# Moving GpSimd's k and q scalings, the FFN's weight sums and two k scalings in a fused attention and FFN kernel

## The chip, the cores and the metric

The kernel runs on one core of a Trainium2 chip. A core has a matrix engine (TensorE, PE in the profile, with its weight loads as PEld), a vector engine (VectorE, DVE), a scalar engine (ScalarE, ACT), a general engine (GpSimd, POOL) and a queue engine (SyncE, SP), each with an instruction stream of its own; they wait for one another through semaphores. The metric is the time of one execution on the device in microseconds (us).

## The reference

Inputs are q, k and v of 4 batches, 8 heads, 768 positions and 64 columns, a decay `lam` for each head, and three weight matrices. First comes an attention without softmax, whose weights decay with distance and whose state is carried from block to block:

```
for b in range(nb):                      # blocks of positions
    intra = (qb @ kb.T * Dmask) @ vb     # Dmask[i, j] = lam ** (i - j) for i >= j, else 0
    inter = (qb * lam_pow) @ kv_state
    out[block] = intra + inter
    kv_state = lam_block * kv_state + (kb * rev_pow).T @ vb
```

Its output, as x of 3072 tokens by 512 columns, goes through a bilinear feed-forward layer (FFN): `a = x @ w_a`, `b = x @ w_b` (512 by 1536 each), and the result is `(a * b) @ w_out` (1536 by 512).

## The kernel before

**Units and groups.** The work is cut into 24 units of 128 positions (4 batches, 6 blocks each). `GROUPS = (4, 2, 4, 4, 4, 4, 2)` says how many units make up one group; the FFN runs group by group. While the FFN of one group runs, the attention pieces of the next units are put between its matmuls.

**Attention of a unit.** Loads of q and k as float32 (`load_x`, line 143), of v as bfloat16 (`make_vb`, line 282, on GpSimd's queue). k and q are multiplied by powers of the decay (`make_ks`, `make_qs`, `scale`, line 266), which takes the place of the decay mask; for units 4 to 7 VectorE scales k, for later units GpSimd does, and q is always GpSimd's. `prep_k` (a step "P") does both scalings; from unit 10 on it also issues a transposing DMA on SP (line 291), calls `pump`, and the step issues the load of v. `pump` issues on SP the loads of q and k for units 10 and up, three units ahead, and first of all, once, waits on SP for v of unit 9 with a tiny copy (line 188). Units 4 to 9 are transposed by TensorE instead (`piece_T`, a step "T", line 302: eight transposes, q's four first, then k's four; ScalarE copies the result, line 304). `piece_S` ("S") computes scores (line 316) and multiplies them by a triangular mask on VectorE (line 333). `piece_V` ("V") and `kv_beside` add to the state (line 380, 402), and VectorE copies it (line 413). `pieces_O` ("O2", "Q") computes the output of two units (line 350), ScalarE writes it as x transposed (line 373), and for the last unit of a group `sums` follows.

**The FFN.** Group 0 uses `ffn`: for each of 12 blocks of 128 features, four matmuls for a, four for b, and a product a·b on VectorE (line 483); then the output matmuls (line 634) into four accumulators. The a blocks of features 8 to 11 are all computed before the first of their b blocks. Groups 1 to 6 use `ffn_seven`: a and b for two halves of the tokens are computed with seven products of half-size matrices instead of eight (line 524). That takes four sums of the weights for each of six column blocks (`w_sums`, a step "TW", lines 489 to 492, VectorE, both inputs in SBUF) and four sums of x for each group (`sums`, lines 502 to 505, VectorE, both inputs in SBUF). Snapshots of the accumulators go through ScalarE (line 539), sums over them through VectorE (558, 569, 575) and for some steps GpSimd (561), and the product a·b of one half of the tokens is GpSimd's (571), of the other VectorE's (578).

**The order.** The schedule is written by hand: the order of the calls is the order of each engine's instructions. `hook(slot)` is called at numbered places of each group's FFN and carries out the steps that `PLAN[group]` lists for that slot. In group 0, slots 0 to 11 come after each feature block's product, slots 12 to 35 after each pair of output matmuls. In the later groups, slots 0 to 11 lie between the seven-product steps, and slots from 12 on between the output matmuls. Slot 6 of group 1 comes after the group's third product of line 571; slot 1 of group 2 before the group's first product of line 571, slot 3 after it, slots 4 and 5 both between its second and third. A step "L" issues loads on GpSimd's queue. The outputs of groups 0 and 1 (units 0 to 5) are kept in SBUF (`o_kept`) and stored in group 2.

**Loads.** GpSimd issues first the weights in the order of `W_ORDER`, mixed with q, k and v of units 4 and 5, and later those of units 6 to 9 in steps "L". Each of its DMA issues keeps GpSimd for 0.7 to 0.9 us.

Of the kernel before, what the change touches and what calls it, by code (L numbers as in the profile page):

```python
# [17 lines left out]
BF16 = mybir.dt.bfloat16  # L18
# [4 lines left out]
def _bc(ap, dims):  # L23
# [19 lines left out]
W_ORDER = ("a0", "a1", "b0", "b1", "a2", "b2", "a3", "b3", "a4", "a5", "b4", "b5", "o0", "q4", "k4", "o1", "v4",  # L43
           "q5", "k5", "o2", "v5", "o3")
PLAN = {
    0: [(0, "V", 3), (1, "TW", 0), (3, "TW", 1), (5, "TW", 2), (7, "TW", 3),
        (9, "P", 4), (9, "L", ("q6", "k6", "o4")), (11, "P", 5), (11, "L", ("o5", "v6", "q7")),
        (12, "L", ("k7", "v7")), (13, "TW", 4), (14, "T", 4), (17, "S", 4), (17, "P", 6), (18, "T", 5),
        (18, "L", ("q8", "k8", "v8")), (21, "V", 4), (22, "S", 5), (23, "TW", 5), (24, "T", 6),
        (24, "L", ("q9", "k9")), (25, "P", 7), (25, "L", ("v9",)), (26, "O2", (4, 5)), (28, "S", 6), (31, "T", 7),  # L50
        (33, "P", 8)],
    1: [(0, "V", 6), (1, "S", 7), (2, "T", 8), (2, "P", 9), (4, "O2", (6, 7)),
        (5, "S", 8), (5, "T", 9), (7, "S", 9), (11, "V", 8), (12, "O2", (8, 9)), (14, "P", 10), (15, "P", 11)],
    2: [(1, "P", 12), (4, "P", 13), (7, "P", 14), (11, "S", 10), (11, "S", 11), (12, "P", 15),
        (14, "P", 16), (17, "P", 17)],
    3: [(4, "P", 18), (7, "P", 19), (13, "P", 20), (16, "P", 21)],
    4: [(4, "P", 22), (7, "P", 23)],
# [9 lines left out]
def kernel(  # L67
# [11 lines left out]
    nc = tc.nc  # L79
    B, H, S, D = q.shape  # L80
    BLK = 128
    NB = S // BLK
# [5 lines left out]
    KS = d_model // 128  # L88
# [3 lines left out]
    singles = ctx.enter_context(tc.tile_pool(name="singles", bufs=1))  # L92
    wst_pool = ctx.enter_context(tc.tile_pool(name="wst", bufs=13))
    ld_pool = ctx.enter_context(tc.tile_pool(name="ld", bufs=4))
    prep_pool = ctx.enter_context(tc.tile_pool(name="prep", bufs=6))
# [37 lines left out]
    raw = {}  # L133

    def load_x(w, u, queue):
        b, nb = divmod(u, NB)
        if u in (n0 + 4, n0 + 5):
            if (u, "kq") not in raw:
                raw[u, "kq"] = wst_pool.tile([128, 2, H, D], F32, name="qkf", tag="wst")
            t = raw[u, "kq"][:, "qk".index(w)]  # L140
        else:
            t = ld_pool.tile([128, H, D], F32, name=w + "f", tag=w + "f", bufs=4)
        queue.dma_start(out=t, in_={"q": qr, "k": kr}[w][b, nb])
        raw[u, w] = t
# [23 lines left out]
    n0 = GROUPS[0]  # L168
# [4 lines left out]
    def load_all(parts):  # L173
        for kind, c in parts:
            if kind in "abo":
                load_w(kind, int(c))
            elif kind == "v":
                make_vb(int(c))
            else:
                load_x(kind, int(c), nc.gpsimd)  # L180

    landed = singles.tile([1, 1], BF16, name="landed")

    def pump():
        if used["u"] < n0 + 6:
            return
        if used["u"] == n0 + 6:
            nc.sync.dma_start(out=landed, in_=U[n0 + 5]["vb"][0:1, 0, 0:1])
        while pending:
            w, u = pending[0]  # L190
            if u >= used["u"] + 3:
                return
            load_x(w, u, nc.sync)
            pending.pop(0)
# [15 lines left out]
    for w, src in (("q", q), ("k", k)):  # L210
# [3 lines left out]
        for c in range(0, HP, n_c):  # L214
            t = wst_pool.tile([128, 1024], F32, name=w + "4", tag="wst")[:, :n_c * 512]
            t = t.rearrange("p (c b x) -> p c b x", c=n_c, b=2)
# [28 lines left out]
    lp_q = singles.tile([128, NT, H, 1], F32, name="lp_q")  # L245
    lp_k = singles.tile([128, NT, H, 1], F32, name="lp_k")
# [12 lines left out]
    U = {}  # L259
    kv = {}  # L260

    def eng_of(name):
        return nc.gpsimd if name == "pool" else nc.vector

    def scale(eng, dst, x, lp):
        eng_of(eng).tensor_mul(dst.rearrange("p (c b) d -> p b c d", b=2),  # L266
                               x[:].rearrange("p (b c) d -> p b c d", b=2),
                               lp.rearrange("p (b c) o -> p b c o", b=2)
                               .to_broadcast([128, 2, HP, D]))

    def make_ks(u, eng):
        qk = prep_pool.tile([128, 2, H, D], BF16, name="qk", tag="qk")
        scale(eng, qk[:, 1], raw.pop((u, "k")), lp_k[:, u % NB])
        U.setdefault(u, {}).update(qk=qk, kn=qk[:, 1])

    def make_qs(u, eng):
        scale(eng, U[u]["qk"][:, 0], raw.pop((u, "q")), lp_q[:, u % NB])

    def make_vb(u):
        b, nb = divmod(u, NB)  # L280
        vb = prep_pool.tile([128, H, D], BF16, name="vb", tag="vb", bufs=8)
        nc.gpsimd.dma_start(out=vb, in_=vr[b, nb])  # L282
        U.setdefault(u, {})["vb"] = vb

    def prep_k(u):
        make_ks(u, "dve" if u < n0 + 4 else "pool")
        make_qs(u, "pool")
        used["u"] = u + 1
        if u in DMA_T:
            qkT = qkT_pool.tile([128, 2, HP, 128], BF16, name="qkT", tag="qkT")  # L290
            nc.sync.dma_start_transpose(
                out=qkT[:].rearrange("p j hp i -> p (j hp) i"),
                in_=U[u]["qk"][:].rearrange("p j h d -> p (j h d)"))
            U[u]["qT"], U[u]["kT"] = qkT[:, 0], qkT[:, 1]
        pump()
# [50 lines left out]
    def o_mm(u, b, c, **ops):  # L346
        h = 4 * b + c
        p = slice(64 * (h % 2), 64 * (h % 2) + 64)
        new = U[u]["flags"]
        nc.tensor.matmul(U[u]["o"][b][p, c // 2, :], start=new[b, h % 2], stop=True,  # L350
                         skip_group_check=True, **ops)
        new[b, h % 2] = False
# [8 lines left out]

    def intra(u, b):
        for c in range(HP):
            o_mm(u, b, c, lhsT=U[u]["vb"][:, 4 * b + c, :], rhs=U[u]["m"](b, c))

    def evac_o(us, b, eng="act"):
        xT, col = xTs[us[0]]
# [9 lines left out]
    def kv_mms(ps, w, cs, first):  # L377
        d = U[w]
        for c in cs:
            nc.tensor.matmul(ps[:, c, :, :], lhsT=d["kn"][:, 2 * c:2 * c + 2, :],  # L380
                             rhs=d["vb"][:].rearrange("p (b c) d -> p c b d", b=2)[:, c],
                             start=(first and c == 0), stop=True, skip_group_check=True)

    def kv_bank():
# [3 lines left out]
    def kv_update(u):  # L388
        if u % NB == NB - 1:
            return  # L390
        if u % NB == 0:
            kv_bank()
        kv_mms(kv["ps"], u, range(HP), u % NB == 0)

    def kv_beside(u):
        if u % NB == 0 or u % NB == NB - 1:
            kv_update(u)
            return
        for c in range(HP):
            for b in range(2):  # L400
                p = slice(64 * b, 64 * b + 64)
                nc.tensor.matmul(kv["ps"][p, c, b, :], lhsT=U[u]["kn"][:, 2 * c + b, :],
                                 rhs=U[u]["vb"][:, 4 * b + c, :],
                                 start=False, stop=True, skip_group_check=True)

    def kv_copy(u, ps, eng="dve"):
# [9 lines left out]
    def piece_S(u):  # L416
        masks(u, scores(u))
# [198 lines left out]
    def store_kept():  # L616
        row, o_sb = kept.pop(0)
        nc.sync.dma_start(out=out_r[row], in_=o_sb)
# [61 lines left out]
    def new_xT(g):  # L680
        gx[g] = xT_pool.tile([128, KS, 512], BF16, name="xT", tag="xT")
        for i in range(GROUPS[g]):
            xTs[g_u0[g] + i] = (gx[g], i * BLK)
# [62 lines left out]
    for u in range(n0):  # L746
        U[u] = dict(kn=kn4[:, u], qT=xT4["q"][:, :, u * BLK:(u + 1) * BLK],
                    m=lambda i, hp, u=u: ms4[hp // 2, u // 2][i][:, 2 * (u % 2) + hp % 2, :])
# [57 lines left out]
    bank["held"].clear()  # L806
    used["u"] = n0
    pump()

    for g, n in enumerate(GROUPS):  # L810
        if g + 1 < len(GROUPS):
            new_xT(g + 1)
        plan = {}
        for slot, name, us in PLAN.get(g, ()):
            plan.setdefault(slot, []).append((name, us))

        def hook(slot, plan=plan):
            for name, us in plan.get(slot, ()):
                if name == "P":
                    prep_k(us)  # L820
                    if us in DMA_T:
                        make_vb(us)
                elif name == "L":
                    load_all(us)
                elif name == "TW":
                    w_sums(us)
                elif name == "W":
                    store_kept()
                elif name == "T":
                    piece_T(us)  # L830
                elif name == "S":
                    piece_S(us)
                elif name == "V":
                    piece_V(us)
                elif name == "O":
                    pieces_O((us,))
                elif name == "O2":
                    pieces_O(us)
                else:
                    pieces_O(us[:2], us[2:])  # L840

        if g in S_GROUPS:
            ffn_seven(g, g_u0[g], n, gx.pop(g), hook, g + 1 == len(GROUPS))
        else:
            ffn(g_u0[g], n, gx.pop(g), hook, g == 0)
# [29 lines left out]
```

## Time and profile before

| What | Value |
|---|---|
| Median of 5 runs | 223.96 us (223.80 to 224.42) |
| Profiled execution, its time | 224.41 us |
| Profiled execution, its span | 222.4 us |
| TensorE busy | 216.0 us (97%) |
| VectorE busy | 154.5 us (69%) |
| GpSimd busy | 136.1 us (61%) |
| ScalarE busy | 104.8 us (47%) |

The profile is of one execution, and its times count from the start of the span. A line of a timeline gives the start, the duration, the engine, the line of the kernel, the operation, output and inputs by the program's names with their shapes, the number of instructions merged into the line, and in brackets how long the engine had been idle and what ended that. A line of waits gives who waited for whom: the sum in us, the number of times, the longest. Group 0's FFN runs from about 17.9 to 53.4 us, group 1's from there to 73.4, group 2's begins at 73.41.

### The profile page before, as it was taken

Reading aid. Unit: us, or ns where it says so; the run is one execution under the profiler, and the core shown is the slowest. Engines: PE = TensorE matmul, PEld = TensorE weight load, DVE = VectorE, ACT = ScalarE, POOL = GpSimd, SP = SyncE. Lnnn points to the kernel's source line nnn. Section 1 sums busy time; section 2 is a strip of 40 time slices with the busy share of each in tenths; the row PEclk is TensorE's granted clock in tenths of the full one; section 3 lists DMA queues with packets and bytes.
Section 4 is the critical chain, followed back from the end, with each engine's and each line's share of the span. In section 5 each row is a group of like instructions: output and inputs, shape, how many; then the busy total and the mean of one; then the engine's idle time right before and its main releaser. Section 6 shows DMA issues by size and latency. Waiting matters only on the chain.

```text
span 222.4 us, 5431 instructions
## 1 busy us (share of the span) xinstructions
PE 216.0 (97%) x2203; PEld 149.5 (67%) x2203; DVE 154.5 (69%) x250; ACT 104.8 (47%) x185; POOL 136.1 (61%) x150
## 2 busy tenths in 40 slices
PE   7899999999999899999999999999999999999994
PEld 2476444556985588754688754688754788745974
DVE  0992997899687987993677873577973687830760
ACT  2686233336862456324466424566324557342622
POOL 6879659996759869995169992169910246400230
PEclk9999999999999999999999999999999999999999
DMA  3999999996753999999977959506611200012102
GB/s 106 312 164 193 202 245 236 227 242 112 177 113 26 173 228 193 201 343 187 277 179 110 174 132 229 115 1 74 71 48 49 97 1 0 3 47 97 47 3 94
DMA packets 82858, 30.76 MB, mean 138 GB/s; under 512 B 70034, under 2 KB 79122, under 8 KB 82834
## 3 DMA queue, kind: packets, MB, share of 16 engines
q0 software_dynamic: 32864, 11.01, 44.2%
q1 hardware_dynamic: 49682, 19.34, 35.6%
q8 instruction: 17, 0.28, 0.5%
q10 hardware_dynamic: 288, 0.07, 0.1%
q14 instruction: 7, 0.06, 0.1%
HBM read 28.32 MB, written 6.29 MB: 156 GB/s over the span
## 4 chain that ended last, share of the span: by engine, by line
PE 88%; DMA 4%; DVE 2%; ACT 2%; SPq 1%; issue 1%; ACTq 0%
PE op L634 25%; PE m_q L524 23%; PE m_r L524 12%; PE m_p L524 6%; PE o_ps L350 5%; PE a_ps L456 5%; PE b_ps L456 5%; PE kq L316 3%; DMA k<-in_k_dram 3%; PE kvd L380 1%; PE tps L302 1%; SPq L218 1%; DVE xs L502 1%; DMA out_dram<-o_sb 1%; ACT o_kept L625 1%
## 5 line engine op out<-in xcount | busy, mean ns | idle before, releaser
L634 PE MATMUL op<-wo_sb,ab 128*128 128x512 bf16 (+2 forms) x312 | 68.1, 363 | 0.0
L571 POOL TENSOR_TENSOR ab<-c,c 128x512 bf16<-128x512 bf16 x30 | 34.8, 1164 | 36.4 <-DVE c L569 35.6
L524 PEld LDWEIGHTS <-tw 128*128 128x128 bf16 x576 | 49.1, 98 | 6.9 <-DVE xs L503 0.4
L634 PEld LDWEIGHTS <-ab 128*128 128x128 bf16 x312 | 27.6, 98 | 26.3 <-POOL ab L571 0.6
L524 PE MATMUL m_q<-xs,tw 128*128 128x256 bf16 (+1 forms) x288 | 36.1, 255 | 0.4 <-ACT s L539 0.2
L561 POOL TENSOR_TENSOR c<-s 128x512 bf16<-128x512 f32 x11 | 14.0, 1272 | 33.9 <-ACT s L539 33.9
L333 DVE TENSOR_TENSOR m<-kq,lotri 128x512 bf16<-128x512 f32 x47 | 29.8, 683 | 5.5 <-PE kq L316 4.9
L629 ACT COPY o_sb<-op 128x512 f32<-128x512 f32 (+2 forms) x20 | 10.9, 543 | 43.5 <-PE op L634 43.0
L578 DVE TENSOR_TENSOR ab<-c,m_q 128x512 bf16<-128x512 f32 x30 | 20.6, 686 | 11.7 <-PE m_q L524 9.8
L524 PEld LDWEIGHTS <-wa_sb 128*128 128x128 bf16 x288 | 24.5, 98 | 3.1
L539 ACT COPY s<-m_q 128x512 f32<-128x512 f32 x30 | 17.6, 588 | 15.7 <-PE m_q L524 14.6
L569 DVE TENSOR_TENSOR c<-u,m_r 128x512 f32<-128x512 f32 x30 | 20.4, 681 | 4.7 <-ACT u L539 4.6
L282 POOL DMA_DIRECT2D vb<-in_v_dram x24 | 22.3, 931 | 1.7 <-DMA wo_sb<-in_moe_w_out_dram 1.1
L558 DVE TENSOR_TENSOR c<-s,m_p 128x512 bf16<-128x512 f32 x19 | 13.0, 686 | 11.8 <-PE m_p L524 11.6
L575 DVE TENSOR_TENSOR c<-s,m_q 128x512 f32<-128x512 f32 x30 | 20.5, 685 | 0.5
L539 ACT COPY s<-m_r 128x512 f32<-128x512 f32 x30 | 17.7, 590 | 6.4 <-PE m_r L524 6.4
L539 ACT COPY u<-m_q 128x512 f32<-128x512 f32 x30 | 17.9, 597 | 5.6 <-PE m_q L524 5.6
L266 POOL TENSOR_TENSOR qk<-qf,lp_q 128x512 bf16<-128x512 f32 x18 | 19.5, 1086 | 0.0
L524 PE MATMUL m_r<-xs,wb_sb 128*128 128x256 bf16 (+1 forms) x144 | 18.1, 255 | 0.9 <-DVE xs L505 0.9
L524 PE MATMUL m_q<-xT,wa_sb 128*128 128x256 bf16 (+1 forms) x144 | 18.1, 255 | 0.0
L524 PE MATMUL m_r<-xs,tw 128*128 128x256 bf16 (+1 forms) x144 | 18.1, 255 | 0.0
L524 PE MATMUL m_q<-xT,tw 128*128 128x256 bf16 (+1 forms) x144 | 18.1, 255 | 0.0
(87 smaller groups left out, 289.3 us busy)
## 6 DMA issues: line engine op xcount, KB each, us to landing
out_dram<-o_sb SPq DMA_DIRECT2D x17, 256.0 KB, 2.0
qf<-in_q_dram SPq DMA_DIRECT2D x14, 256.0 KB, 4.5
kf<-in_k_dram SPq DMA_DIRECT2D x14, 256.0 KB, 4.9
vb<-in_v_dram POOLq DMA_DIRECT2D x24, 128.0 KB, 4.9
wa_sb<-in_moe_w_a_dram POOLq DMA_DIRECT2D x6, 256.0 KB, 6.8
wb_sb<-in_moe_w_b_dram POOLq DMA_DIRECT2D x6, 256.0 KB, 7.8
wo_sb<-in_moe_w_out_dram POOLq DMA_DIRECT2D x6, 256.0 KB, 7.3
out_dram<-o_kept SPq DMA_DIRECT2D x6, 256.0 KB, 3.8
```

Of the source, the lines that this page charges most:

```text
L266: eng_of(eng).tensor_mul(dst.rearrange("p (c b) d -> p b c d", b=2), x[:].rearrange("p (b c) d -> p b c d", b=2), lp.rearrange("p (b c) o ...
L282: nc.gpsimd.dma_start(out=vb, in_=vr[b, nb])
L333: nc.vector.tensor_mul(m, kq[i], lotri_bc)
L456: nc.tensor.matmul(ps[:, lo:hi], lhsT=w_sb[:, s, f * 128:(f + 1) * 128], rhs=xT[:, s, lo:hi], start=(s == 0), stop=(s == KS - 1), skip_gro ...
L524: nc.tensor.matmul(ps[:, f, :], lhsT=w(k, f), rhs=x[:, k, :], start=(first and f == 0 and k == 0), stop=True, skip_group_check=True)
L539: nc.scalar.copy(t, ps)
L561: nc.gpsimd.tensor_add(d["c11"], d["s12"][:, 0], d["s12"][:, 1])
L569: nc.vector.tensor_add(c12, d["u2"], d["r"])
L571: nc.gpsimd.tensor_mul(ab[:, nf * i:nf * i + nf, 0:h], d["c11"], c12)
L575: nc.vector.tensor_add(d["c22"], d["s5"], d["q"])
L578: nc.vector.tensor_mul(ab[:, nf * i:nf * i + nf, h:2 * h], d["c22"], d["q"])
L634: nc.tensor.matmul(op[:, lo:hi], lhsT=ab[:, f, t * 128:(t + 1) * 128], rhs=wo_sb[:, f, lo:hi], start=(f == 0), stop=(f == FC - 1))
```

## The change

`PLAN` of groups 0, 1 and 2 is rearranged, and a few helpers are split so that k and q of a unit can be scaled at different places.

- The weight sums 4 and 5 ("TW") move from slots 13 and 23 of group 0 to slots 7 and 8.
- Unit 7's scalings ("P") move from slot 25 to 23 of group 0.
- Units 8 and 9 are no longer prepared by "P" (slot 33 of group 0, slot 2 of group 1). GpSimd scales their q at slots 23 and 30 ("QS"), VectorE their k at slots 29 and 33 ("KS"), and what followed the scaling in `prep_k` (now `scaled`, with `pump`) comes with "KS".
- q and k of unit 9 are loaded through SP at slot 22 ("LS"), behind a wait for k of unit 7, instead of through GpSimd at slot 24; v of unit 9 at slot 23 instead of 25.
- Unit 9's transposition moves from slot 5 to 3 of group 1, unit 10's "P" from slot 14 to 6 of group 1, unit 12's from 1 to 3 and unit 13's from 4 to 5 of group 2.

```diff
 PLAN = {
-    0: [(0, "V", 3), (1, "TW", 0), (3, "TW", 1), (5, "TW", 2), (7, "TW", 3),
+    0: [(0, "V", 3), (1, "TW", 0), (3, "TW", 1), (5, "TW", 2), (7, "TW", 3), (7, "TW", 4), (8, "TW", 5),
         (9, "P", 4), (9, "L", ("q6", "k6", "o4")), (11, "P", 5), (11, "L", ("o5", "v6", "q7")),
-        (12, "L", ("k7", "v7")), (13, "TW", 4), (14, "T", 4), (17, "S", 4), (17, "P", 6), (18, "T", 5),
-        (18, "L", ("q8", "k8", "v8")), (21, "V", 4), (22, "S", 5), (23, "TW", 5), (24, "T", 6),
-        (24, "L", ("q9", "k9")), (25, "P", 7), (25, "L", ("v9",)), (26, "O2", (4, 5)), (28, "S", 6), (31, "T", 7),
-        (33, "P", 8)],
-    1: [(0, "V", 6), (1, "S", 7), (2, "T", 8), (2, "P", 9), (4, "O2", (6, 7)),
-        (5, "S", 8), (5, "T", 9), (7, "S", 9), (11, "V", 8), (12, "O2", (8, 9)), (14, "P", 10), (15, "P", 11)],
-    2: [(1, "P", 12), (4, "P", 13), (7, "P", 14), (11, "S", 10), (11, "S", 11), (12, "P", 15),
+        (12, "L", ("k7", "v7")), (14, "T", 4), (17, "S", 4), (17, "P", 6), (18, "T", 5),
+        (18, "L", ("q8", "k8", "v8")), (21, "V", 4), (22, "S", 5), (22, "LS", 9), (23, "P", 7), (23, "QS", 8),
+        (23, "L", ("v9",)), (24, "T", 6), (26, "O2", (4, 5)), (28, "S", 6), (29, "KS", 8),
+        (30, "QS", 9), (31, "T", 7), (33, "KS", 9)],
+    1: [(0, "V", 6), (1, "S", 7), (2, "T", 8), (3, "T", 9), (4, "O2", (6, 7)), (5, "S", 8), (6, "P", 10),
+        (7, "S", 9), (11, "V", 8), (12, "O2", (8, 9)), (15, "P", 11)],
+    2: [(3, "P", 12), (5, "P", 13), (7, "P", 14), (11, "S", 10), (11, "S", 11), (12, "P", 15),
...
-    landed = singles.tile([1, 1], BF16, name="landed")
+    def wait_for(t):
+        landed = singles.tile([1, 1], t.dtype, name="landed")
+        nc.sync.dma_start(out=landed, in_=t[0:1, 0, 0:1])
...
-            nc.sync.dma_start(out=landed, in_=U[n0 + 5]["vb"][0:1, 0, 0:1])
+            wait_for(vbs[n0 + 5])
...
     def prep_k(u):
         make_ks(u, "dve" if u < n0 + 4 else "pool")
         make_qs(u, "pool")
+        scaled(u)
+
+    def scaled(u):
         used["u"] = u + 1
...
+                elif name == "QS":
+                    make_qs(us, "pool")
+                elif name == "KS":
+                    make_ks(us, "dve")
+                    scaled(us)
+                elif name == "LS":
+                    wait_for(raw[us - 2, "k"])
+                    load_x("q", us, nc.sync)
+                    load_x("k", us, nc.sync)
```

The remaining lines of the diff let `make_qs` run before `make_ks` (the unit's tile is made by whichever comes first) and keep the v tiles in a dictionary of their own, `vbs`.

## The prediction

> **What bounds the kernel now.** I read the page first, then who waits on TensorE, then the timelines of TensorE, VectorE and GpSimd around the two stretches in which the change moves work. The page says where the time is:
>
> ```profile
> span 222.4 us, 5431 instructions
> PE 216.0 (97%) x2203; PEld 149.5 (67%) x2203; DVE 154.5 (69%) x250; ACT 104.8 (47%) x185; POOL 136.1 (61%) x150
> ```
>
> TensorE is busy for 216.0 of 222.4 us at a granted clock of 1.00 in every slice, and nearly all of the rest lies before its first and after its last matmul. So the order of TensorE's instructions is the path, and another engine counts only where TensorE stands still for it. The view of waits on TensorE names these places from 20 us on:
>
> ```profile
> PE m_r L524 <- DVE xs L505: 0.9, 1, 0.9
> PE m_q L524 <- ACT s L539: 0.2, 1, 0.2
> PE m_q L524 <- DVE xs L503: 0.2, 1, 0.2
> ```
>
> Two of the three are waits for VectorE's sums of x (lines 502 to 505) at the start of group 2. TensorE's timeline there:
>
> ```profile
> 73.84 0.60 PE L524 MATMUL m_r<-xs,tw 128*128 128x256 bf16 x4
> 74.28 0.60 PE L524 MATMUL m_p<-xT,wa_sb 128*128 128x256 bf16 x4
> 75.05 0.61 PE L524 MATMUL m_q<-xs,tw 128*128 128x256 bf16 x4 [0.17 <-DVE xs L503]
> 76.57 0.61 PE L524 MATMUL m_r<-xs,wb_sb 128*128 128x256 bf16 x4 [0.91 <-DVE xs L505]
> ```
>
> Such blocks of four start 0.44 us apart when nothing is waited for (73.84 to 74.28). The third is due at 74.72 and starts at 75.05, 0.33 us late; the fourth is due at 75.49 and starts at 76.57, 1.08 us late. Together 1.41 us: that is all the sums of x cost TensorE. Now VectorE's and GpSimd's timelines of the same stretch:
>
> ```profile
> 70.81 2.46 DVE L502 TENSOR_TENSOR xs<-xT 128x512 bf16<-128x512 bf16 x1 [1.26 <-ACT xT L373]
> 73.30 1.69 DVE L503 TENSOR_TENSOR xs<-xs,xT 128x512 bf16<-128x512 bf16 x1
> 74.92 1.26 DVE L504 TENSOR_TENSOR xs<-xT 128x512 bf16<-128x512 bf16 x1
> 76.10 0.41 DVE L505 TENSOR_TENSOR xs<-xT,xs 128x512 bf16<-128x512 bf16 x1
> ```
>
> ```profile
> 70.70 1.05 POOL L266 TENSOR_TENSOR qk<-kf,lp_k 128x512 bf16<-128x512 f32 x1
> 71.71 1.04 POOL L266 TENSOR_TENSOR qk<-qf,lp_q 128x512 bf16<-128x512 f32 x1
> 72.70 0.94 POOL L282 DMA_DIRECT2D vb<-in_v_dram  x1
> 73.65 1.05 POOL L266 TENSOR_TENSOR qk<-kf,lp_k 128x512 bf16<-128x512 f32 x1
> 74.66 1.23 POOL L266 TENSOR_TENSOR qk<-qf,lp_q 128x512 bf16<-128x512 f32 x1
> ```
>
> A sum that takes 0.42 us alone (0.41 at 76.10) takes 2.46 us beside two scalings, 1.69 beside a DMA issue and a scaling, 1.26 beside a scaling. Each ends about one free sum after GpSimd's scaling does: an operation of VectorE with both inputs in SBUF is held for the whole of a GpSimd scaling, and the reverse (1.23 for the last, 1.04 for a free one). VectorE's products with one input in PSUM keep 0.68 us throughout.
>
> **The sums of x in group 2: −1.41 us.** The scalings at 70.70 are unit 11's, those at 73.65 unit 12's. Unit 11's stay: between slots 6 and 14 of group 1 neither GpSimd nor SP has an instruction, so unit 10 moved from slot 14 to 6 keeps its place behind the third product of line 571 in both queues, its V load, transposing DMA and next two loads too, and unit 11 follows at once. The first sum still ends near 73.2. Unit 12 (slot 1 to 3) goes behind group 2's first product. The second sum then meets only unit 11's V load and ends between 73.7 (at once) and 74.1 (after the issue); the other two end by 74.8. TensorE wants the second at 74.72 and the last at 75.16. Both waits go; next in line is nothing of VectorE's. GpSimd pays: its first product of group 2 starts near 76.65, and behind it come without a gap 5 more products (1.13 each by spacing), 1 sum (1.36), and units 12, 13, 14 at 2.94 (two scalings and an issue): 76.65 + 6×1.13 + 3×2.94 + 1.36 = 93.6. The output product that reads the last of these starts at 95.35 − 1.41 = 93.94, so 0.3 us of cover is left; without it the cost is what the chain is late. Unit 13 (slot 4 to 5) passes no GpSimd instruction.
>
> **The weight sums inside the first FFN step: +1.50 us.** Sums 4 and 5, eight operations, move from 40.21 and 46.69 to behind sum 3 and behind the product of feature block 8. Their weights have landed by 30.9 (landings in the trace). The rows there, VectorE, then GpSimd, then TensorE:
>
> ```profile
> 33.76 1.26 DVE L492 TENSOR_TENSOR tw<-wa_sb,tw 128x512 bf16<-128x512 bf16 x1
> 36.34 0.69 DVE L483 TENSOR_TENSOR ab<-a_sb,b_ps 128x512 bf16<-128x512 bf16 x1 [1.32 <-PE b_ps L456]
> 37.20 0.69 DVE L483 TENSOR_TENSOR ab<-a_sb,b_ps 128x512 bf16<-128x512 bf16 x1 [0.18 <-PE b_ps L456]
> 37.81 0.68 DVE L266 TENSOR_TENSOR qk<-kf,lp_k 128x512 bf16<-128x512 f32 x1
> ```
>
> ```profile
> 34.60 1.31 POOL L266 TENSOR_TENSOR qk<-qf,lp_q 128x512 bf16<-128x512 f32 x1
> 38.40 1.08 POOL L266 TENSOR_TENSOR qk<-qf,lp_q 128x512 bf16<-128x512 f32 x1
> ```
>
> ```profile
> 39.95 0.61 PE L302 MATMUL tps<-ident,qk 128*128 128x128 bf16 x8
> ```
>
> The k scaling of unit 4 ends at 38.49, and TensorE transposes it from 39.95 on (q first, k from 40.17). It is queued on VectorE behind all eight moved sums. A set of four takes 1.47 us by start spacing (32.63 to 34.10 without the hold). Set 4 starts at 34.95 during GpSimd's q scaling of unit 4: its first sum ends near 36.2 instead of 35.4, the set gives way at 37.25; product 8 takes 0.60 to 37.85; two sums of set 5 pass until 38.65, then GpSimd's q scaling of unit 5, held since 38.40, takes its 1.0 us; the other two end near 40.3; product 9 to 40.9; the k scaling of unit 4 to 41.6. TensorE's k transposes start at about 41.67 instead of 40.17: 1.50 us in which all of TensorE stands. Bounds: if the sum at 33.76 runs freely, set 4 mostly fits the old 1.32 us gap and set 5 passes before 38.75; then only the k scaling itself is held to 40.43, a stall of 0.33; without any hold it ends at 39.83, no stall. At the other end GpSimd's DMA issues hold sums too, as one seems to at 46.69, where a weight sum took 1.15 us beside nothing but issues: one such hold adds 0.73, for 2.2. I take 1.50, because it repeats the holds of this very stretch. Nothing later is late again: k of unit 5 ends near 43.5, wanted at 42.78 + 1.5.
>
> The Trainium skill (SBUF — State Buffer, Who interferes with whom) states that a VectorE instruction with two SBUF inputs contends with a GpSimd instruction that reads SBUF, whole instructions long; the rows at 70.81 and 34.60 agree. It infers that such an instruction does not contend with GpSimd's descriptor writing; the row at 46.69 speaks otherwise. By the rule the stall here ends at 1.50; by the row it may reach 2.2.
>
> **The rest: 0.** K of units 8 and 9 on VectorE: two operations of 0.68 at slots 29 and 33 (VectorE free of 2.9 us of weight sums and 3.2 us of holds since 40 us). Unit 9's wait on SP: k of unit 7 lands at 47.25, so q and k of unit 9 are issued at about 48.1 and 48.7 and land, at the 4.5 and 4.9 us that the page gives SP's loads, at 52.6 and 53.6 (now 52.5 and 53.3). Behind that wait on SP stand only these loads and, after V of unit 9 has landed (54.45), the six loads for units 10 to 12, as now. Q of unit 9 on GpSimd waits until 52.6 with nothing behind it before 56.35. K of unit 9 on VectorE may wait to 53.6, with the state copy (54.96) and masks (56.31) behind it; their readers on TensorE come after 61. The GpSimd issues removed (1.81 us at 47.62) let unit 7's and 8's q end near 50.4, and V of unit 9 is issued as before. The sums of group 1 (1.62, 1.36, 1.12, 0.28 from 49.57) shrink to about 1.1 us, but TensorE waits for none of them: its 0.39 us at 54.95 belong to ScalarE, whose copies at 52.74 keep their order. Unit 9's transposition (slot 5 to 3) needs the same 0.45 us of TensorE and 1.0 us of ScalarE, which has about 0.2 us there; the snapshots around it are read later. Its bounds are −0.1 and +0.1.
>
> **The sum.** The profiled execution took 224.41 us, a span of 222.40 and 2.01 around it, 0.45 above the median of the runs. 224.41 − 1.41 + 1.50 = 224.50.
>
> **The rivals.** (A) *The holds fall kindly*: VectorE's eight sums slip past GpSimd's two scalings and the stall is under 1.0 us. For it: 1.32 us of idle VectorE at 35.02, and 1.46 us between k's end and its transposition. Against: both scalings stand in the middle. With 0.33 the time is 223.33, with none 223.00; it decides once the stall is below 0.96, the gain less 0.45 us. (B) *The DMA issues hold the sums as well*: six of them lie between 35 and 42 us. For it the 1.15 at 46.69; against it, the sums at 40.21 to 41.34 kept 0.42 beside two issues. With 2.2, 225.2. (C) *The change doesn't do what it says in group 2*: unit 11 stays, and a second sum held past 74.72 or a late GpSimd chain leaves only half of the gain: 224.41 − 0.7 + 1.5 = 225.2.
>
> **How the numbers follow.** Forecast (stall 1.0 to 2.0, so 224.0 to 225.0) 0.46, A 0.33, B 0.14, C 0.07. About 0.2% (0.45 us) is what a measurement of this kernel can tell from no change: 223.51 to 224.41. Of the forecast 0.17 lies within and 0.29 above; of A 0.28 is below and 0.05 within; B and C are above. Faster 0.28, same 0.22, slower 0.50. The range takes in A without a stall and B with a little more, 222.9 to 225.6; the forecast's own is 224.0 to 225.0.
>
> **What would show it.** Right: no wait on the sums of x at group 2; two or three weight sums near 35 and 38.5 of 1 us or more; k of unit 4 ending past 41 and a gap of TensorE at 40; GpSimd without idle time in group 2. Wrong: that gap under 0.5 us, or an xs wait left, or a gap at unit 9's transposition.

## The result, and the profile after

The changed kernel takes 225.23 us (median of 43 runs), the kernel before 224.06 us (80 runs): a ratio of 1.0049, 95% interval 1.0039 to 1.0060. It is slower by half a per cent. The forecast was 224.5 us: its direction and its range (222.9 to 225.6) hold, and its time is 0.7 us too small. Taken as a change it is further off, as the account of its sum below says. A ratio here is not the quotient of two medians: the kernel before has some executions near 225.8 us, which move the ratio and hardly the median, so the two can differ by some 0.3%. The profiled execution after took 225.84 us with a span of 224.1; the one before 224.41 us with 222.4. The first lines of the page of after:

```profile
span 224.1 us, 5434 instructions
PE 214.9 (96%) x2203; PEld 149.3 (67%) x2203; DVE 151.9 (68%) x252; ACT 104.5 (47%) x185; POOL 132.1 (59%) x146
```

VectorE and GpSimd have less to do than before (154.5 and 136.1 us then), TensorE has the same 2203 matmuls, and the span is longer. Fewer busy microseconds on engines that are not the path (the chain of work that sets the time) have bought nothing; the waits of TensorE say why. The waits on TensorE of after, from 20 us on (who waited for whom, the sum in us, how many, the longest):

```profile
PE tps L313 <- DVE ab L494: 1.4, 1, 1.4
PE m_p L535 <- ACT o_sb L640: 0.5, 1, 0.5
PE o_ps L361 <- DVE st L424: 0.4, 1, 0.4
PE m_q L535 <- ACT s L550: 0.2, 1, 0.2
PE tps L313 <- DVE qk L268: 0.2, 1, 0.2
```

Both waits for the sums of x are gone. In their place stand waits for product 9 and for the k scaling, ahead of unit 4's transposition; for a state copy; and for an output buffer. The wait for ScalarE's snapshot (0.2) was there before. The line numbers have moved by some ten: the scaling is line 268, the sums of the weights 500 to 503, the sums of x 513 to 516, the product a·b 494, the output copy 640.

**Unit 4's transposition.** TensorE's timeline of before, at the first output matmul, and of after:

```profile
38.66 1.46 PE L634 MATMUL op<-wo_sb,ab 128*128 128x512 bf16 x6
```

```profile
38.35 1.46 PE L645 MATMUL op<-wo_sb,ab 128*128 128x512 bf16 x6
41.22 0.38 PE L313 MATMUL tps<-ident,qk 128*128 128x128 bf16 x4 [1.42 <-DVE ab L494]
41.83 0.40 PE L313 MATMUL tps<-ident,qk 128*128 128x128 bf16 x4 [0.22 <-DVE qk L268]
```

The output matmuls start 0.31 us earlier than before (38.35 against 38.66), so the transposes of q were due at 39.64 and those of k four transposes, 0.22 us, after them. They start at 41.22 and 41.83: 1.58 and another 0.39 us late, 1.97 us together. VectorE's timeline of after shows what they waited for, and GpSimd's shows why VectorE was late:

```profile
33.78 2.12 DVE L500 TENSOR_TENSOR tw<-wb_sb,wa_sb 128x512 bf16<-128x512 bf16 x1
35.94 0.42 DVE L501 TENSOR_TENSOR tw<-wb_sb,tw 128x512 bf16<-128x512 bf16 x1
...
36.61 1.26 DVE L503 TENSOR_TENSOR tw<-wa_sb,tw 128x512 bf16<-128x512 bf16 x1
37.80 0.68 DVE L494 TENSOR_TENSOR ab<-a_sb,b_ps 128x512 bf16<-128x512 bf16 x1
38.40 1.04 DVE L500 TENSOR_TENSOR tw<-wb_sb,wa_sb 128x512 bf16<-128x512 bf16 x1
...
40.49 0.68 DVE L494 TENSOR_TENSOR ab<-a_sb,b_ps 128x512 bf16<-128x512 bf16 x1
41.09 0.68 DVE L268 TENSOR_TENSOR qk<-kf,lp_k 128x512 bf16<-128x512 f32 x1
```

```profile
33.84 0.70 POOL L163 DMA_DIRECT2D wo_sb<-in_moe_w_out_dram  x1
34.55 1.06 POOL L268 TENSOR_TENSOR qk<-qf,lp_q 128x512 bf16<-128x512 f32 x1
...
36.47 0.90 POOL L143 DMA_DIRECT2D kf<-in_k_dram  x1
...
38.06 1.09 POOL L268 TENSOR_TENSOR qk<-qf,lp_q 128x512 bf16<-128x512 f32 x1
```

A free sum takes 0.42 us (35.94). Three of the eight moved ones are held: the first for 2.12 us, through GpSimd's DMA issue and the scaling behind it; the one at 36.61 for 1.26, beside nothing but an issue; the one at 38.40 for 1.04, beside the second scaling. VectorE has no pause between 33.78 and the end of the k scaling at 41.77.

**Group 2.** VectorE's timeline of after at the sums of x:

```profile
72.87 2.23 DVE L513 TENSOR_TENSOR xs<-xT 128x512 bf16<-128x512 bf16 x1 [1.26 <-ACT xT L384]
75.14 0.42 DVE L514 TENSOR_TENSOR xs<-xs,xT 128x512 bf16<-128x512 bf16 x1
75.48 0.42 DVE L515 TENSOR_TENSOR xs<-xT 128x512 bf16<-128x512 bf16 x1
75.82 0.42 DVE L516 TENSOR_TENSOR xs<-xT,xs 128x512 bf16<-128x512 bf16 x1
```

Unit 11's scalings still hold the first sum; the other three are free (1.69, 1.26 and 0.41 us before). TensorE passes the stretch from group 2's first block to the block behind the sums in 2.25 us, where it took 3.61. Its timeline of before, then of after, at these two blocks:

```profile
73.41 0.60 PE L524 MATMUL m_q<-xT,wa_sb 128*128 128x256 bf16 x4
...
77.02 0.60 PE L524 MATMUL m_q<-xT,wa_sb 128*128 128x256 bf16 x4
```

```profile
75.47 0.60 PE L535 MATMUL m_q<-xT,wa_sb 128*128 128x256 bf16 x4
...
77.72 0.60 PE L535 MATMUL m_q<-xT,wa_sb 128*128 128x256 bf16 x4
```

**Where the time went.** Last matmul against last matmul, the two profiled executions differ by 1.42 us. Another 0.28 us of the span lies behind it, and the time outside the span is 0.27 us shorter (1.74 against 2.01). The places, by how late TensorE is at each: start −0.31; unit 4's transposition +1.97; the state copy at 71.07 +0.45; the sums of x −1.36; the output buffer at 110 +0.68. The sum is +1.43. The start is no effect of the change: kernel 6 below does up to there what the kernel before does, and its first output matmul comes at 38.20 instead of 38.66.

### The profile page after: what moved, and what is told of

Same layout as the page of the kernel before. It is cut to its first block, busy times and chain, and to the rows that moved or that the text cites. A ratio compares the mean times of both kernels' runs of the same rounds, so it can differ in the third digit from the quotient of the medians.

```text
span 224.1 us, 5434 instructions
## 1 busy us (share of the span) xinstructions
PE 214.9 (96%) x2203; PEld 149.3 (67%) x2203; DVE 151.9 (68%) x252; ACT 104.5 (47%) x185; POOL 132.1 (59%) x146
## 4 chain that ended last, share of the span: by engine, by line
PE 74%; DMA 12%; DVE 5%; ACT 3%; issue 2%; SPq 1%; POOL 1%; ACTq 0%; DVEq 0%
PE op L645 25%; PE m_q L535 23%; PE m_r L535 11%; PE m_p L535 6%; PE o_ps L361 4%; DMA kf<-in_k_dram 4%; DMA wa_sb<-in_moe_w_a_dram 3%; DMA out_dram<-o_sb 3%; DMA k<-in_k_dram 3%; PE kq L327 2%; DVE tw L500 2%; SPq L220 1%; PE tps L313 1%; ACT o_kept L636 1%; PE kvd L391 1%
## 5 line engine op out<-in xcount | busy, mean ns | idle before, releaser
L268 POOL TENSOR_TENSOR qk<-qf,lp_q 128x512 bf16<-128x512 f32 x18 | 18.9, 1051 | 0.0
L535 PE MATMUL m_p<-xT,wa_sb 128*128 128x256 bf16 (+1 forms) x144 | 18.1, 255 | 0.5 <-ACT o_sb L640 0.5
L384 ACT CAST xT<-o_ps 128x512 bf16<-128x512 f32 x22 | 11.9, 588 | 13.5 <-PE o_ps L361 13.3
```

The costliest lines, as they stand in the source:

```text
L535: nc.tensor.matmul(ps[:, f, :], lhsT=w(k, f), rhs=x[:, k, :], start=(first and f == 0 and k == 0), stop=True, skip_group_check=True)
```

## The experiments

All times are medians; ratios are against the kernel before, with 95% intervals. Two questions are asked: is the loss that of the weight sums, and what are the two small waits that the prediction had not named?

**1. The weight sums put back.** In the kernel after:

```diff
-    0: [... (7, "TW", 3), (7, "TW", 4), (8, "TW", 5),
+    0: [... (7, "TW", 3),
-        ... (14, "T", 4), ... (23, "P", 7), (23, "QS", 8),
+        ... (13, "TW", 4), (14, "T", 4), ... (23, "TW", 5), (23, "P", 7), (23, "QS", 8),
```

> The changed kernel with weight sums 4 and 5 back at slots 13 and 23 of group 0, the rest of the change kept. Theory (the sums, held by GpSimd, stand in front of unit 4's k scaling and TensorE waits 1.97 us for it): TensorE's two gaps at unit 4's transposition go, its next gap over 0.3 us is ScalarE's 0.40 at the start of group 1, the sums of x stay short, and the time falls by about 2.0 us, from 225.2 to 223.2. Rival (the sums only move their trouble: set 5 at slot 23 meets the q scalings of units 7 and 8, and then the transposition or the sums of group 1 are late): 224.4 or more, with a new gap of TensorE between 46 and 57 us.

Measured: 223.86 us, 0.9978 (0.9959 to 0.9997), 1.37 us below after. Both gaps at unit 4's transposition are gone; the waits for the state copy and the output buffer stay. So the moved sums make the gap, and they are the larger part of the loss. The time falls by less than the 2.0 us expected. In this profiled execution TensorE gains the 1.97 us and comes to the output matmuls 0.27 us later than in that of after (38.62), and the wait for the output buffer is 0.14 us longer. The stall itself is not one number either: in the profiles with the sums at slots 7 and 8 it is 1.97 (after), 1.98 (kernel 2), 1.24 (kernel 3) and 2.14 us (kernel 5).

**2. Unit 9's transposition put back.** In the kernel after:

```diff
-    1: [(0, "V", 6), (1, "S", 7), (2, "T", 8), (3, "T", 9), (4, "O2", (6, 7)), (5, "S", 8), (6, "P", 10),
+    1: [(0, "V", 6), (1, "S", 7), (2, "T", 8), (4, "O2", (6, 7)), (5, "S", 8), (5, "T", 9), (6, "P", 10),
```

> The changed kernel with unit 9's transposition back at slot 5 of group 1. Theory (its 0.45 us of TensorE, now ahead of the third sum's product, push VectorE's chain from that product to the state copy of unit 8, for which TensorE's output product waits 0.61 us late at 70.4): the wait falls to about the 0.16 of before and the time to 224.8. Rival (the copy is late because VectorE has the k scalings of units 8 and 9): the wait stays at 0.6 and the time at 225.2.

Measured: 224.89 us, 1.0028 (1.0006 to 1.0050). The medians fall by 0.34, but the intervals of this kernel and of after overlap, so the time alone decides nothing. The traces do. TensorE's timeline of after, and then of this kernel, at the output piece that reads the state copy:

```profile
71.07 0.31 PE L361 MATMUL o_ps<-qkT,st 64*64 64x128 bf16 x8 [0.45 <-DVE st L424]
```

```profile
70.21 0.61 PE L361 MATMUL o_ps<-qkT,st 64*64 64x128 bf16 x16
```

The eight and eight matmuls run together again; how late the second eight are falls from 0.61 to 0.16 us, as before the change. The wait at 41 us is unchanged. So unit 9's earlier transposition costs 0.45 us in the trace. In the traces one can follow how: it puts 0.45 us of TensorE ahead of a product (62.66 before, 64.72 after, 2.06 later, where the work behind the transposition's old place is 1.61 later), VectorE begins its chain behind that product 0.45 us later, and the chain has no pause up to the state copy (70.34).

**3. A fourth output buffer.** In the kernel after; the second edit is there to make room for it in SBUF:

```diff
-    o_pool = ctx.enter_context(tc.tile_pool(name="o", bufs=3))
+    o_pool = ctx.enter_context(tc.tile_pool(name="o", bufs=4))
-    loglam = singles.tile([128, H], F32, name="loglam")
+    loglam = lam_sb
```

> The changed kernel with four output buffers instead of three (the logarithm of the decay is written in place to make room). Theory (unit 12's later transposing DMA pushes SP's stores back, the first store of group 2 lands at 109.8, ScalarE's fourth copy waits 3.6 us for its buffer, and TensorE 0.68 us for ScalarE): ScalarE's wait for the store goes, TensorE's gap at 110 falls to the 0.04 of before, the time to about 224.5. Rival (the stores and loads are all late from the load on the DMA engines, and the next transfer is waited for instead): the gap moves and the time stays at 225.2.

Measured: 224.73 us, 1.0030 (1.0010 to 1.0051), a median 0.50 below after, with intervals that overlap. The gap at 110 us is gone. ScalarE's timeline of after, and of this kernel, at the fourth output copy of group 2:

```profile
109.92 0.58 ACT L640 COPY o_sb<-op 128x512 f32<-128x512 f32 x1 [3.60 <-DMA out_dram<-o_sb]
```

```profile
108.07 0.59 ACT L640 COPY o_sb<-op 128x512 f32<-128x512 f32 x1 [2.44 <-PE op L645]
```

After, this copy waits for the store of the first output to leave its buffer; with a fourth buffer it waits only for its matmul. Why the store is late shows in SP's queue, after and then before:

```profile
82.07 1.23 SPq L302 DMA_TRANSPOSE qkT<-qk  x1
...
95.11 3.94 SPq L629 DMA_DIRECT2D out_dram<-o_kept  x6
...
103.76 1.87 SPq L641 DMA_DIRECT2D out_dram<-o_sb  x1
```

```profile
78.39 2.69 SPq L291 DMA_TRANSPOSE qkT<-qk  x1
...
92.02 4.32 SPq L618 DMA_DIRECT2D out_dram<-o_kept  x6
...
99.62 3.27 SPq L630 DMA_DIRECT2D out_dram<-o_sb  x1
```

Unit 12's transposing DMA is issued 3.68 us later, since unit 12 is scaled later, and all that stands behind it on SP in order comes later too: the kept outputs by 3.09, the first output's store by 4.14. Some 0.7 of this is the whole kernel being later (77.02 to 77.72 behind the sums of x), and the last 1.05 us come from issues on SP that take longer (q and k behind the kept outputs 1.17 and 1.60, before 0.58 and 0.93).

What the wait costs, the time of this kernel doesn't show. The 0.50 is not the buffer's alone: in this profiled execution the stall at unit 4's transposition is 0.73 us shorter as well. And the wait is not always there: of the six profiles with unit 12 at slot 3 and three buffers, after and kernels 1, 6 and 7 have it, 2 and 8 do not. In those two the first store lands 4.6 us behind its issue, in the other four 5.4 to 6.1.

The edit also comes with something that it was not made for. In the five profiles with four buffers (kernels 3, 4, 9, 10 and 11) k of unit 9 lands, by the trace's record of landings, between 55.4 and 55.9 us, in the eight with three between 51.8 and 53.9. Why is open.

**4. All three at once**: the edits of 1, 2 and 3 together in the kernel after.

> The three together: weight sums back at slots 13 and 23, unit 9's transposition back at slot 5, four output buffers; kept of the change are the scalings of units 7 to 9 and 12, and unit 9's loads through SP. Theory (the terms add): 225.2 - 2.0 - 0.45 - 0.65 = 222.1, that is 1.9 us under the kernel before: the 1.36 us of the sums of x and nothing lost, and some of the start. If the terms add but the start is what it was: 222.7. Rival (the gains overlap, since a TensorE that runs ahead meets GpSimd's or a DMA's next limit): 223.5 or more.

Measured: 222.94 us, 0.9940 (0.9927 to 0.9953). The three savings, 1.37 + 0.34 + 0.50 = 2.21, come near the 2.29 by which this kernel lies below after. A new gap of 0.38 us appears. VectorE's timeline of this kernel, then TensorE's:

```profile
55.87 0.69 DVE L268 TENSOR_TENSOR qk<-qkf,lp_k 128x512 bf16<-128x512 f32 x1 [2.27 <-DMA qkf<-in_k_dram]
```

```profile
59.60 0.61 PE L535 MATMUL m_q<-xT,tw 128*128 128x128 bf16 x8 [0.21 <-DVE c L586]
```

VectorE stands for 2.27 us until k of unit 9 lands (55.84), and from there works without a pause up to the sum that TensorE waits for. In the kernel after, k landed at 52.80 and TensorE began group 1 at 55.04, 1.78 us later than here. It is not TensorE's lateness alone that covered for the scaling there: in kernel 1 TensorE is as early as here (53.34 against 53.26), k lands at 53.94, and the sum is done at 58.75, while the block that waits for it could start at 59.31 at the earliest, even without unit 9's transposition ahead of it. What kernel 4 has and kernel 1 has not is the late landing, which all profiles with the fourth buffer share. The three repairs without that edit were not run.

**5. Only the weight sums moved**, in the kernel before:

```diff
-    0: [... (5, "TW", 2), (7, "TW", 3),
+    0: [... (5, "TW", 2), (7, "TW", 3), (7, "TW", 4), (8, "TW", 5),
-        ... (13, "TW", 4), (14, "T", 4), ... (22, "S", 5), (23, "TW", 5), (24, "T", 6),
+        ... (14, "T", 4), ... (22, "S", 5), (24, "T", 6),
```

> The kernel before with one part of the change alone: weight sums 4 and 5 at slots 7 and 8 of group 0. Theory (they stand in front of unit 4's k scaling and are held by GpSimd): TensorE's gap at unit 4's transposition, 1.2 to 2.0 us, the waits on the sums of x at group 2 as before, time 224.1 + 1.6 = 225.7. Rival (the gap comes from the parts together, for instance from GpSimd's other order): no gap, 224.1.

Measured: 225.88 us, 1.0062 (1.0029 to 1.0095), 1.76 above before. The profiled execution was the longest of the ten, 227.84 us, for a reason of its own that stands in the last section. The waits on the sums of x are as before. The stall is 2.14 us here, and part of it comes from the k scaling of unit 4 itself, which takes 1.50 us for 0.68 beside nothing but DMA issues:

```profile
40.43 1.50 DVE L266 TENSOR_TENSOR qk<-kf,lp_k 128x512 bf16<-128x512 f32 x1
```

**6. Only units 12 and 13 moved**, in the kernel before:

```diff
-    2: [(1, "P", 12), (4, "P", 13), (7, "P", 14), (11, "S", 10), (11, "S", 11), (12, "P", 15),
+    2: [(3, "P", 12), (5, "P", 13), (7, "P", 14), (11, "S", 10), (11, "S", 11), (12, "P", 15),
```

> The kernel before with units 12 and 13 alone moved (slots 1 and 4 of group 2 to 3 and 5). Theory (unit 12's scalings are all that the sums of x of group 2 lose time to beyond what TensorE covers): the two waits for the sums of x fall from 1.41 to 0.1 us at most, SP's stores come 3 us later and cost up to 0.7 us at 108 us; time between 222.8 and 223.5. Rival (the gain needs units 8 and 9 off GpSimd as well): a wait on the sums of x of over 0.5 us stays, 223.6 or more.

Measured: 222.57 us, 0.9900 (0.9862 to 0.9938), 1.55 below before and a little below the range expected. VectorE's timeline of this kernel:

```profile
70.35 2.25 DVE L502 TENSOR_TENSOR xs<-xT 128x512 bf16<-128x512 bf16 x1 [1.26 <-ACT xT L373]
72.63 0.42 DVE L503 TENSOR_TENSOR xs<-xs,xT 128x512 bf16<-128x512 bf16 x1
```

The sums run as in after, with no other edit: the whole gain of the change is in these two slot numbers. The profiled execution shows the wait for an output buffer too. From the waits on TensorE:

```profile
PE m_p L524 <- ACT o_sb L629: 0.7, 1, 0.7
```

That execution took 223.54 us, the other five 222.47 to 222.75. That the wait comes in some executions of this order of work and not in others, the profiles named under 3 show; that these five lacked it is inferred from their times.

**7. Is it the transposition's place in the queue?** In the kernel after, weight sum set 5 goes behind unit 5's scalings and so behind the k scaling of unit 4:

```diff
-    0: [... (7, "TW", 3), (7, "TW", 4), (8, "TW", 5),
-        ... (11, "P", 5), (11, "L", ("o5", "v6", "q7")),
+    0: [... (7, "TW", 3), (7, "TW", 4),
+        ... (11, "P", 5), (11, "TW", 5), (11, "L", ("o5", "v6", "q7")),
```

> The changed kernel with weight sums 5 behind unit 5's k scaling (slot 11, behind its P) instead of slot 8; sums 4 stay at slot 7. Theory (set 5, with its hold by the q scaling of unit 5, is what makes unit 4's k late; set 4 mostly fits into VectorE's idle time): k of unit 4 ends by 39.9, TensorE's gap there is under 0.5 us, time 225.2 - 1.6 = 223.6. Rival (set 4, held by the q scaling of unit 4, is enough): gap of 1 us or more, 224.4 or more.

Measured: 224.60 us, 0.9999 (0.9969 to 1.0029). Neither expectation was right as written. There is no gap at the transposition, but VectorE's timeline shows where the holds went:

```profile
41.50 1.26 DVE L500 TENSOR_TENSOR tw<-wb_sb,wa_sb 128x512 bf16<-128x512 bf16 x1
...
43.47 1.34 DVE L503 TENSOR_TENSOR tw<-wa_sb,tw 128x512 bf16<-128x512 bf16 x1
44.74 1.27 DVE L344 TENSOR_TENSOR m<-kq,lotri 128x512 bf16<-128x512 f32 x2
```

The set now stands in front of unit 4's masks, two of its four sums are held, and TensorE waits for the masks at 44.5 to 46.1, 0.78 and 0.55 us late. The place in the queue decides which reader waits; the holds decide how long.

**8. Are GpSimd's scalings the cause of the holds?** In the kernel after, GpSimd fills q of units 4 and 5 with a constant, which writes SBUF and reads nothing. The q scaling of these two units is left out.

```diff
+        if u in (n0, n0 + 1):
+            raw.pop((u, "q"))
+            nc.gpsimd.memset(qk_of(u)[:, 0], 0.5)
+            return
         scale(eng, qk_of(u)[:, 0], raw.pop((u, "q")), lp_q[:, u % NB])
```

> The changed kernel with GpSimd's q scalings of units 4 and 5 left out: GpSimd fills q of these two units with a constant instead, which reads nothing, so the outputs of these units are not the reference's. Theory A (only a GpSimd operation that reads SBUF holds the sums): all eight weight sums take 0.42 us, k of unit 4 ends by 39.9, no gap of TensorE over 0.2 us there, time 223.3. Theory B (GpSimd's DMA issues hold them too): one or more of the sums takes 0.8 us or more beside nothing but issues, and a gap of 0.4 to 1.2 us stays, time 223.7 to 224.6.

Measured: 223.40 us, 0.9945 (0.9912 to 0.9978), 1.83 below after. VectorE's timeline of this kernel, whose sums stand four lines further on, at the first sums of set 4 and set 5 and at the k scaling:

```profile
33.72 0.42 DVE L504 TENSOR_TENSOR tw<-wb_sb,wa_sb 128x512 bf16<-128x512 bf16 x1
...
36.57 0.42 DVE L504 TENSOR_TENSOR tw<-wb_sb,wa_sb 128x512 bf16<-128x512 bf16 x1
...
38.63 0.68 DVE L268 TENSOR_TENSOR qk<-kf,lp_k 128x512 bf16<-128x512 f32 x1
```

All eight moved sums take 0.42 or 0.43 us, also those beside the fill, the k scaling ends at 39.31 instead of 41.77, and there is no gap. So the eight sums do fit in front of the transposition; what does not fit is their holds, and the holds beside a scaling come from GpSimd reading SBUF. (The fill is also shorter than a scaling, 0.55 and 0.59 us against 1.06 and 1.09.) The holds beside nothing but DMA issues are gone here as well, which the last section comes back to.

**9. Units 12 and 13 moved, with a fourth output buffer**: the edits of 6 and of 3 in the kernel before.

> The kernel before with units 12 and 13 moved and four output buffers (the logarithm of the decay in place, to make room). Theory (what the move of unit 12 costs is ScalarE's wait for an output buffer, a gap of TensorE of 0.90 us at 108 us in the profile of the move alone): the gap falls to 0.05 and the time from 222.6 to between 221.8 and 222.2. Rival (the late stores are waited for elsewhere, or the runs that are not profiled have no such wait): 222.4 to 222.6.

Measured: 222.76 us, 0.9933 (0.9908 to 0.9958). The 221.8 to 222.2 expected did not come. As the rival had it, the median is no better than that of 6, since most executions of 6 seem not to meet the wait; but the longest of the six is 222.95, where 6 had one of 223.54. What is left is ScalarE's 0.40 us at the start of group 1.

**10. Unit 7's transposition two slots earlier**, on top of 9:

```diff
-        ... (26, "O2", (4, 5)), (28, "S", 6), (31, "T", 7),
+        ... (26, "O2", (4, 5)), (28, "S", 6), (29, "T", 7),
```

> As the one with four output buffers, and unit 7's transposition at slot 29 instead of 31 of group 0, ahead of the last output matmuls, so that ScalarE's copy of it is done when group 0's outputs come. Theory (TensorE's 0.40 us at the start of group 1 is ScalarE being late by the transposition's copy of 1.0 us): the gap falls under 0.15 us and the time by 0.3 us. Rival (ScalarE's four output copies of 0.5 us each are enough to be late): the gap stays at 0.3 or more and the time within 0.1 us of the other.

Measured: 222.42 us, 0.9920 (0.9893 to 0.9947): the lowest median of all, below both kernels, though not told apart by these runs from 6 and 9. ScalarE's timeline of this kernel, and of 9, at its copies of the kept outputs:

```profile
51.99 2.05 ACT L625 COPY o_kept<-op 128x512 f32<-128x512 f32 x4 [0.28 <-PE op L634]
```

```profile
52.42 2.06 ACT L625 COPY o_kept<-op 128x512 f32<-128x512 f32 x4
```

In 9 these copies stand behind ScalarE's copy of unit 7's transposes (51.52, 1.01 us). Here that copy is done earlier, the kept outputs wait only for their matmul, and the 0.40 us gap of TensorE is gone.

**11. The weight sums at slots 13 and 14**, in kernel 4, between its places and those of the change:

```diff
-        ... (13, "TW", 4), (14, "T", 4), ... (23, "TW", 5), (23, "P", 7),
+        ... (13, "TW", 4), (14, "T", 4), (14, "TW", 5), ... (23, "P", 7),
```

> The three repairs of the changed kernel (unit 9's transposition back, four output buffers, weight sums out of slots 7 and 8) with the weight sums at slots 13 and 14 instead of 13 and 23. Theory (the repaired kernel's remaining gap of 0.38 us at 59 us, a wait for VectorE, comes from sums 5 and the two k scalings coming together on VectorE between 48 and 56 us): the gap goes and the time falls from 222.9 to 222.5. Rival (the two k scalings alone bring it): the gap stays, 222.9.

Measured: 224.11 us, 0.9986 (0.9961 to 1.0012). The gap at 59 us is gone, as intended, but one sum is held for 1.39 us by GpSimd's scaling at 42.78, and unit 4's masks are late as in 7: TensorE loses 0.74 and 0.55 us there. Neither expectation named this, and it leaves open what made the gap: VectorE still stands 1.67 us for k of unit 9, and TensorE is again over a microsecond later.

## Why the prediction was right, and where it was not

**The sums of x, −1.41.** Right in mechanism and size: 1.36 us in the trace of after, 1.55 in the time of kernel 6 alone. The first sum is still held by unit 11's scalings (2.23), the rest are free. GpSimd's chain in group 2 is without idle time from 78.88 us on; its last product is done at 95.87 and read at 96.05. The cover that the prediction put at 0.3 us held, with 0.2 us left.

**The weight sums, +1.50.** Right in mechanism: held by the scalings of units 4 and 5, k queued behind. The k transposes start at 41.83, where the prediction had 41.67. The stall is 1.97 instead of 1.50 mostly because TensorE came to the transposition 0.31 us earlier in this execution, while GpSimd's scaling of unit 4, on which the holds hang, came as before (34.55 against 34.60). Over four profiles the stall is 1.24 to 2.14 us. By the times, undoing the move gives 1.37 back and making it alone costs 1.76; the estimate lies between. The particular holds were not the predicted ones: the hold at the end of set 3 that the prediction repeated did not come, so set 4 began at 33.78 and not at 34.95, its first sum lost 1.70 us (2.12 for 0.42) where 0.8 had been put down, its last sum lost 0.84 beside an issue (the kind of hold on which rival B rests), and set 5 lost 0.62 instead of 1.0. That the sum came out near is partly luck.

**"Its bounds are −0.1 and +0.1."** This step, on unit 9's transposition, was wrong. It looked at ScalarE's spare time and at the readers of the snapshots. The cost came through VectorE: 0.45 us of TensorE moved ahead of a product, and behind that product VectorE has no pause for five microseconds, at whose end TensorE waits for the state copy (kernel 2). The question "what does this delay, and has that a pause before its own reader" was put to one engine only.

**Unit 12 moved past group 2's first product.** The prediction priced GpSimd's chain and VectorE's sums, and no term stood for SP, though SP's transposing DMA of unit 12 waits for the scaling and six kept outputs and the first output's store wait behind it in order. That cost 0.68 us in the profiled execution of after and 0.89 in that of kernel 6, where nothing else is moved; in the profiles of 2 and 8 it cost nothing, and what it costs in the median the runs do not separate (kernel 3).

**K of units 8 and 9 on VectorE, 0.** True for the kernel after, where k of unit 9 landed at 52.80 (53.6 in the prediction), and for kernel 1, where TensorE is on time. The prediction named the wait ("may wait to 53.6") but took its cover from readers after 61 us; what stands closer is the sum that a block due at 59.2 waits for. With k landing at 55.84 that block came 0.38 us late (kernel 4).

**The sum.** By its own terms the prediction had a change of +0.09 (−1.41 + 1.50); between the profiled executions it is +1.43. The difference of 1.34 is the start −0.31, the stall +0.47, the state copy +0.45, the sums of x +0.05 and the output buffer +0.68: most of it in two terms that the prediction put at nothing or did not have, the rest in the size of the stall and in the start. The medians say the same less sharply: +1.17 was measured, and changes made or undone alone give 1.76 − 1.55 + 0.34 + 0.50 = +1.05. That the time came out only 0.73 us too small, past the forecast's own 224.0 to 225.0 but within the wider range, is partly luck: the sum started from an execution of 224.41, which lies 0.35 above the median of the 80 runs before. Rival A did not come, C did not come, and B came in part: the time is the one that it gave, 225.2, but after has one hold of its kind and a stall of 1.97 instead of 2.2, and the rest of the time comes from elsewhere.

## What to carry to other kernels

Moving a scaling out of the way of other work moves everything that the same step issues: here the two slot numbers of units 12 and 13 gained 1.55 us, and what took part of it back in some executions was the store queue behind the step's transposing DMA, on an engine that neither part of the argument was about. When several edits come together, price each at the place where its delay ends, not at the engine it is made on, and try them one at a time: here the kernel with two edits and a side effect of the third undone lies 2.29 us below after, more than the third had gained. And a repair is an edit like any other: the fourth buffer took away a wait for a store, and with it came loads that land some 2 us later, so look at what else moved before the next gap is put down to the change under study.

## What the runs showed of the hardware

**The granted clock can fall after a short gap.** In kernel 5's profiled execution the gap at the transposition was 0.94 and 1.20 us, and then the clock dropped. The view of stretches (stretch, its length, busy time and instructions of TensorE, weight loads, VectorE, ScalarE, GpSimd, the granted clock, DMA share, GB/s):

```profile
40.00:42.00 2.00, 0.40 (x5) 0.23 (x5) 2.00 (x3) 0.00 (x0) 2.00 (x4) 1.00 1.20 203
42.00:44.00 2.00, 1.78 (x7) 0.91 (x9) 2.00 (x3) 1.01 (x1) 2.00 (x3) 0.53 1.70 242
44.00:46.00 2.00, 2.00 (x14) 0.72 (x13) 0.77 (x2) 0.00 (x0) 2.00 (x3) 0.62 1.61 241
46.00:60.00 14.00, 13.66 (x160) 8.43 (x161) 7.26 (x15) 7.85 (x13) 6.90 (x8) 1.00 0.89 172
```

TensorE works 0.40 of the 2 us from 40, and gets 0.53 and 0.62 of its clock in the next 4, which is (0.47 + 0.38) × 2 = 1.7 of the 2.0 us by which this execution is longer than the median. In this one a stall of 2.1 us cost nearly twice its length. It does not always: the 1.97 us in the profiled execution of after left the mean clock at 1.000. A mean clock of 0.992, as here, is on record for 4 of the 78 executions of the kernels with this stall (after, 2, 3 and 5; after's are its two longest, 227.48 and 228.61 us) and for none of the 145 of the kernel before and the other experiments. The other three were not profiled, so that the stall led to it there is inferred. The Trainium skill (TensorE: Matmul & The Clock Gate, Part 1: The HAM clock gate) says that the clock falls after at least one idle window of some 3.4 us. In this run 2.1 us of gap, with four transposes inside, was enough.

**Holds beside DMA issues.** Over ten profiles (before, after and kernels 1 to 8), VectorE's weight sums, sums of x and k scalings, whose inputs are both in SBUF, were held in 50 of 71 cases beside a GpSimd scaling, never in 214 cases beside nothing, and in 8 of 249 beside GpSimd's DMA issues without a scaling (in five of the 249 beside kernel 8's fill too), by 0.6 to 0.85 us each. The last kind is the one that rival B supposed. The Trainium skill (SBUF — State Buffer, Who interferes with whom) lets such an instruction contend with a GpSimd instruction that reads SBUF, not with one that only writes it; kernel 8, where the fill held nothing, agrees. In each of the eight, GpSimd had done a scaling two or three instructions earlier, and kernel 8 shows no such hold in 33 cases; at 3 in 100, that many cases would often show none. What causes these eight is left open. Open too is why the hold at 33.78 in after began during the issue ahead of the scaling and not with it; the sum at 33.76 before, counted above as beside a scaling, even ended (35.02) well before that scaling did (35.91).
